# A recurrence regrouped: units of 64 tokens of four batches in place of 128 tokens of two, with the small products at fixed places

## The chip, the core and the metric

The kernel runs on one core of a Trainium2 chip, in one launch. The metric is device time in microseconds (us). The core has five engines with instruction queues of their own: TensorE (PE in the profile, its weight loads PEld) for matrix products and transposes, VectorE (DVE) and ScalarE (ACT) for elementwise work, GpSimd (POOL), and SyncE (SP), which issues most DMAs. An engine runs its instructions in program order; it waits where one needs a result that another engine or a DMA has not made yet. TensorE writes to PSUM, a small memory of eight banks; everything else lies in SBUF or in DRAM.

## The reference

Two stages: a delta-rule attention over 768 tokens (4 batches, 8 heads, head size 48), and a feed-forward layer with a squared ReLU over the 4 x 768 = 3072 tokens that come out of it.

```python
k_n = k / (np.linalg.norm(k, axis=-1, keepdims=True) + 1e-06)
state = np.zeros((B, H, D, D))                       # B, H, D = 4, 8, 48
for t in range(S):                                   # S = 768
    kt, vt, bt = (k_n[:, :, t], v[:, :, t], beta[:, :, t, None])
    y[:, :, t] = np.einsum('bhd,bhde->bhe', q[:, :, t], state)
    v_old = np.einsum('bhde,bhd->bhe', state, kt)
    state = state + bt[:, :, :, None] * np.einsum('bhd,bhe->bhde', kt, vt - v_old)

x = y.transpose(0, 2, 1, 3).reshape(B * S, H * D)    # 3072 x 384
h = np.maximum(x @ w_in, 0.0)                        # w_in 384 x 2048
out = (h * h) @ w_out                                # w_out 2048 x 384
```

All data is float32. The tokens of one batch depend on one another through the state (48 x 48 a head and batch); batches and heads are independent, and the feed-forward layer needs only the rows of its own tokens.

## The kernel before, in words

**The recurrence in chunks.** 64 tokens are taken at once. With K, Q, V of a chunk and the state S at its start, the kernel forms the products K K^T and Q K^T (masked to the strict triangle), solves a unit triangular system for U from V - K S, and then has y = Q S + (masked Q K^T) U and S + K^T U. The triangular matrix is inverted in two blocks of 32 tokens: both diagonal blocks by elimination on VectorE, the block below them by two small products.

**Units.** A unit is a piece of 256 token rows on which all of this is done at once; there are twelve. Before, a unit is 128 tokens of two batches: two chunks one after the other (c = 0, 1), and units of the two batch pairs take turns (u // 2 is the token tile, u % 2 the pair), with a state tile for each pair. Rows of a tile are 2 batches x 64 tokens or, where heads stand there, 2 heads x 64.

**The parts of a unit.** Each is a Python generator that issues instructions up to its next `yield`:
- `loads`: DMAs of keys, queries, beta and values for units ahead, and the norm of the keys (`normalize`, L277 on ScalarE, L278 on VectorE);
- `static`: transposes of keys and queries on TensorE (L324) and their copies by ScalarE to `kq` (L327); the products (L340), masked by VectorE into `ap` (L350); the diagonal blocks out to DRAM (`blocks`, L358) and back in another layout (`lt`, L366), on SyncE's queue;
- `invert`: 31 rounds of two VectorE instructions (L429, L430) on `lt` and `z`, one factor at the end (L432), then `z` out to DRAM (`inv`, L436) and back into the tiles `tt` (L445) and `t1t` (L450);
- `whole`: the two small products that make the inverse's lower block (L468, L476), with a VectorE transpose of `t1t` (L461) ahead and ScalarE copies behind (L470, L480);
- `sequential`, for each of the two chunks: the products of keys and queries with the state (L498); V - K S on VectorE (L501); the inverse times that (L509), copied by ScalarE (L512); K^T U (L520), added to the state by VectorE (L523), and (Q K^T) U (L528), copied by ScalarE to `y` (L531);
- `moe`: the feed-forward stream of the unit's 256 rows. `y` is transposed on TensorE (L545) and split into a high part `x_h` (ScalarE, L550) and a low part `x_l` (VectorE, L551). Then come steps: nine products of 256 columns into `h` (L581: high x high, high x low, low x high), ReLU, square and high part on ScalarE (L588, L589, L591), the low part `h_l` on VectorE (L560), and steps of six products of 384 columns into `o` (L568). 16 steps of the first and 16 of the second kind make a unit.

Weights come in as float32 and are split once into a high and a low half (`split_weights`: steps on ScalarE, GpSimd, VectorE, two small sums on TensorE, L170 and L171, and a ScalarE copy, L172). 28 pieces of weights are split in the first units, between the other work.

**The order of the work.** The program writes the order of every engine out by hand. Units 0 and 1 are prepared together at the start, with weights split in between; then the loop over u = 1 to 11 issues, mixed with one another by `weave`, the state part of unit u (`whole`, then `sequential`), the stream of unit u - 1, `static` and `invert` for unit u + 1 and the loads of u + 2. `weave` gives the n steps of each part places between two fractions a and b of the unit, sorts all and takes them in turn; between two parts that are not marked "quiet" it pulls one step of the stream ahead:

```python
for x, (gen, n, a, b, *_) in enumerate(parts):
    order += [(a + (b - a) * (m + 0.5) / n, x) for m in range(n)]
...
    if x != filler and not quiet and not apart and filler in order:
        order.remove(filler)
        next(parts[filler][0], None)
```

`invert` is quiet and spreads over 0.40 to 1.12, that is into the next unit. Three steps of a stream (OVER), its copy and its output are left over to the next unit.

PSUM has two banks `g` (the state's products and, in turn, a pair for the transposes and products), two `x` (all other small products; in units 0 and 1 in turn with `h`), two `h` (L581 and the transposes of `y`) and two `o`.

## Time and profile before

| | |
|---|---|
| runs (us) | 688.55, 691.68, 691.93; median 691.68 |
| profiled execution (us) | 693.1, of it the span of the instructions 691.2 |
| granted TensorE clock, mean | 0.96 |
| TensorE busy | 612.2 us, 89% of the span, 9900 products |
| VectorE busy | 435.6 us, 63%, 1175 instructions |
| ScalarE busy | 322.8 us, 47%, 644 instructions |
| GpSimd busy | 75.1 us, 11% |
| DMA | 49.92 MB in 173725 packets |

The profile is one execution, taken by the hardware. A group of instructions is named by its line in the program, its engine and its operation, with out <- in by tile names; then stand the busy time, the mean duration of one in ns and the idle time of that engine just ahead of the group, with what ended it. Rows in order of time start with the time in us from the start of the span and the duration. Products overlap in TensorE's pipeline, so durations of neighbours may overlap too: the pace is read from the starts. "PEclk" is the clock that TensorE was granted, as a share of full speed.

### The profile page before, as it was taken

Reading aid. Unit: us, or ns where it says so; the run is one execution under the profiler, and the core shown is the slowest. Engines: PE = TensorE matmul, PEld = TensorE weight load, DVE = VectorE, ACT = ScalarE, POOL = GpSimd, SP = SyncE. Lnnn points to the kernel's source line nnn. Section 1 sums busy time; section 2 is a strip of 40 time slices with the busy share of each in tenths; the row PEclk is TensorE's granted clock in tenths of the full one; section 3 lists DMA queues with packets and bytes.
Section 4 is the critical chain, followed back from the end, with each engine's and each line's share of the span. In section 5 each row is a group of like instructions: output and inputs, shape, how many; then the busy total and the mean of one; then the engine's idle time right before and its main releaser. Section 6 shows DMA issues by size and latency. Waiting matters only on the chain. (4 is left out here: it accounts for less than half of the span.)

```text
span 691.2 us, 23095 instructions
## 1 busy us (share of the span) xinstructions
PE 612.2 (89%) x9900; PEld 557.1 (81%) x9900; DVE 435.6 (63%) x1175; ACT 322.8 (47%) x644; POOL 75.1 (11%) x90
## 2 busy tenths in 40 slices
PE   0850887879999999999999999999999999999997
PEld 0530456769998988989999989889889899999997
DVE  4789875897468377487486594683774874741121
ACT  3630564753643544544445535435445444454352
POOL 7531431220100100101001001001001010000000
PEclk9966797998999999999999999999999999999999
DMA  7698620500350441531422513505315314030000
GB/s 157 147 222 313 174 45 11 101 8 2 63 113 8 90 90 18 105 60 30 100 53 47 115 22 59 114 9 109 72 18 103 63 30 103 3 62 3 24 1 24
DMA packets 173725, 49.92 MB, mean 72 GB/s; under 512 B 165424, under 2 KB 168504, under 8 KB 173624
## 3 DMA queue, kind: packets, MB, share of 16 engines
q1 hardware_dynamic: 171160, 47.85, 32.8%
q8 instruction: 78, 1.28, 0.8%
q10 hardware_dynamic: 2336, 0.59, 0.4%
q14 instruction: 23, 0.19, 0.1%
q0 software_dynamic: 128, 0.01, 0.0%
HBM read 37.32 MB, written 11.01 MB: 70 GB/s over the span
## 5 line engine op out<-in xcount | busy, mean ns | idle before, releaser
L568 PE MATMUL o<-w,h_h 128*128 128x384 f32 x768 | 204.7, 348 | 0.0
L581 PE MATMUL h<-x_h,w 128*128 128x256 f32 x1152 | 176.2, 289 | 7.5 <-DVE x_l L551 6.1
L560 DVE TENSOR_TENSOR h_l<-r,h_h 128x512 fp32r<-128x512 f32 x96 | 66.6, 694 | 155.6 <-PE o L568 70.4
L581 PEld LDWEIGHTS h<-x_h,w 128*128 128x128 f32 x1152 | 154.6, 191 | 11.8 <-ACT kq L327 5.6
L568 PEld LDWEIGHTS o<-w,h_h 128*128 128x128 f32 x768 | 133.2, 189 | 3.3
L568 PE MATMUL o<-w,h_l 128*128 128x384 f32 x384 | 130.1, 339 | 0.0
L588 ACT ACTIVATE r<-h 128x512 f32<-128x512 f32 x96 | 57.5, 599 | 129.8 <-PE h L581 129.7
L429 DVE SCALAR_TENSOR_TENSOR tmp<-lt,bt,z 128x126 f32<-128x126 f32 (+22 forms) x310 | 95.7, 309 | 26.1 <-DMA lt<-blocks 13.7
L581 PE MATMUL h<-x_l,w 128*128 128x256 f32 x576 | 100.2, 283 | 0.0
L430 DVE TENSOR_TENSOR z<-z,tmp 128x126 f32<-128x126 f32 (+22 forms) x310 | 79.2, 256 | 10.7
L581 PEld LDWEIGHTS h<-x_l,w 128*128 128x128 f32 x576 | 82.8, 191 | 0.0
L568 PEld LDWEIGHTS o<-w,h_l 128*128 128x128 f32 x384 | 72.6, 189 | 0.0
L589 ACT ACTIVATE r<-r 128x512 f32<-128x512 f32 x96 | 60.8, 633 | 3.1
L591 ACT CAST h_h<-r 128x512 fp32r<-128x512 f32 x96 | 59.6, 621 | 3.1
L413 POOL MEMSET z<- 128x512 f32 x10 | 5.3, 531 | 400.9 <-DMA inv<-z 400.9
L512 ACT COPY r<-x 128x192 f32<-128x192 f32 x46 | 12.6, 324 | 72.2 <-PE x L509 72.2
L143 POOL TENSOR_SCALAR a<-a 128x384 f32<-128x384 f32 (+1 forms) x19 | 27.2, 1434 | 49.6 <-ACT a L142 45.0
L550 ACT CAST x_h<-h 128x384 fp32r<-128x384 f32 x24 | 10.4, 486 | 39.8 <-PE h L545 39.8
L498 PEld LDWEIGHTS g<-state,kq 48*64 48x64 f32 x1408 | 23.3, 138 | 5.5 <-issue 5.5
L170 PE MATMUL o<-r,plus 128*128 128x512 f32 (+1 forms) x16 | 10.7, 761 | 17.5 <-DVE r L153 17.5
L509 PEld LDWEIGHTS x<-vt,tt 64*64 64x64 f32 x736 | 15.4, 134 | 13.3 <-issue 8.4
L498 PE MATMUL g<-state,kq 48*64 48x48 f32 x1408 | 26.1, 224 | 0.0
(131 smaller groups left out, 715.2 us busy)
## 6 DMA issues: line engine op xcount, KB each, us to landing
w<-in_moe_w_in_dram SPq DMA_DIRECT2D x12, 512.0 KB
w<-in_moe_w_out_dram SPq DMA_DIRECT2D x16, 384.0 KB
lt<-blocks SPq DMA_DIRECT2D x22, 256.0 KB
vt<-in_v_dram SPq DMA_DIRECT2D x48, 96.0 KB
out_dram<-a SPq DMA_DIRECT2D x46, 96.0 KB
kpad<-in_k_dram SPq DMA_DIRECT2D x88, 48.0 KB
qpad<-in_q_dram SPq DMA_DIRECT2D x88, 48.0 KB
blocks<-ap SPq DMA_DIRECT2D x48, 64.0 KB
```

The costliest lines, as they stand in the source:

```text
L143: nc.gpsimd.tensor_scalar(out=a.bitcast(F32), in0=a.bitcast(F32), scalar1=LEAST, scalar2=None, op0=ALU.max)
L429: nc.vector.scalar_tensor_tensor(out=tmp, scalar=bt[:, s:s + 1], op0=ALU.mult, op1=ALU.mult, **factors)
L430: nc.vector.tensor_tensor(out=z[:, :nj, s + 1:], in0=z[:, :nj, s + 1:], in1=tmp, op=ALU.subtract)
L498: nc.tensor.matmul(dst[to * C:(to + 1) * C, j, p], lhsT=kq[rows, c, p, b, x], rhs=s[rows, b, p], start=(x == 0 and p == 0), stop=False, sk ...
L509: nc.tensor.matmul(tv[j][to, p], lhsT=tt[rows, c, h], rhs=vt[rows, c, h], start=True, stop=True)
L512: nc.scalar.copy(out=uu[:, j::2], in_=tv[j])
L560: nc.vector.tensor_tensor(out=h_l, in0=r, in1=h_h.bitcast(F32), op=ALU.subtract)
L568: nc.tensor.matmul(o[i], lhsT=a[:, e, i * P:(i + 1) * P], rhs=halves["wo", ft][w], start=(ft == 0 and n == 0), stop=(ft == FT - 1 and n == 2))
L581: nc.tensor.matmul(hp[:, e], lhsT=halves["wi", (kt, ft // EACH)][w][:, f], rhs=x[:, kt], start=(n == 0), stop=(n == 3 * KT - 1))
L588: nc.scalar.activation(out=r, in_=hp, func=AF.Relu)
L589: nc.scalar.activation(out=r, in_=r, func=AF.Square)
L591: nc.scalar.copy(out=h_h, in_=r)
```

## The change

A unit becomes 64 tokens of all four batches: `u` is the chunk, and the index that counted the two chunks of a unit (c = 0, 1) now counts two batch pairs (batches 2c + b). The shapes of the tiles for keys, queries, values and products stay as they are; the two state tiles become one with a pair index, and each unit takes one step of the recurrence, in which both pairs go side by side:
- L498 now runs for both pairs at once, 64 products for queries into `g` and 64 for keys into two `x` banks, issued straight behind the first small product (L461; before L468), which goes to an `h` bank; the subtraction is two VectorE instructions of 384 columns;
- `solved` is the product with the inverse (L512) for both pairs, copied back into `vt`;
- `onward` is K^T U (L528), one addition of 384 columns for each half of the state, (Q K^T) U (L537) and two copies to `y`.

The order has fixed places: the stream's 28 steps of its own unit stand at 4/32 to 31/32, the four of the unit before at 0 to 3/32; the four steps of the state part at CHAIN (11.9, 15.9, 19.9, 23.9 of 32); `static` has its first step ahead of the unit and its second at 4.9/32; the transposes of `y` (now one step) stand ahead of everything. The rule that pulls steps ahead is gone. In unit 0 six weights are split beside the state part (2, 1, 2, 1), not seven, so one more is left to unit 1. Tokens, beta and output rows are addressed to match; output and computation are the same. Line numbers shift: L324, L327, L340, L350 become L317, L320, L333, L343; L429, L430, L432 become L422, L423, L425; L468, L476 become L461, L471; L509, L520, L528, L531 become L512, L528, L537, L541; L545, L550, L551, L560 become L554, L557, L558, L567; L568 and L581 become L575 and L588.

```diff
-    state = []
-    for i in range(NU):
-        s = const.tile([P, 2, NP, D], F32, name=f"state{i}")
-        nc.gpsimd.memset(s, 0.0)
-        state.append(s)
+    state = const.tile([P, 2, NC, NP, D], F32, name="state")
+    nc.gpsimd.memset(state, 0.0)
...
-    AHEAD = 20
+    AHEAD = 19
...
     def tokens(x, d):
-        t0, b0 = d["t0"], d["b0"]
-        return [x[b0 + b, :, t0:t0 + P, :].rearrange("h (c t) d -> t c h d", c=NC) for b in range(2)]
+        t0 = d["u"] * C
+        return [x[b::2, :, t0:t0 + C].rearrange("c h t d -> t c h d") for b in range(2)]
...
         nc.vector.transpose(out=t1, in_=d["t1t"])
         m = apool.tile([P, H, HB], F32, name="m", bufs=1)
         at = [upper, lower]
-        ps = x_tile(u)[:, :H * HB].rearrange("p (k t) -> p k t", k=H)
+        ps = ps_h.tile([P, PC], F32, name="h")[:, :H * HB].rearrange("p (k t) -> p k t", k=H)
         for h in range(H2):
             c, e = h // H, h % H
             for b in range(2):
                 nc.tensor.matmul(ps[at[h % 2][b], h // 2], lhsT=ap[lower[b], c, e, 0, :HB], rhs=tt[lower[b], c, e, HB:],
                                  start=True, stop=True)
         nc.scalar.copy(out=m, in_=ps)
+        if u:
+            on_state(d)
         yield
         ps = [x_tile(u)[:, :H * HB].rearrange("p (k t) -> p k t", k=H) for _ in range(2)]
         for h in range(H2):
...
                 nc.scalar.mul(out=right[upper[b], j, :, HB:], in_=ps[j][upper[b]], mul=-1.0)
         yield
...
-    def sequential(d):
...
+    def areas(two, n):
+        return [x[:, :NC * n * D].rearrange("p (c n e) -> p c n e", c=NC, n=n) for x in two]
+    def by_parity(x):
+        return [x.rearrange("p c (n j) e -> p j c n e", j=2)[:, j] for j in range(2)]
+    def on_state(d):
+        kq, vt = d["kq"], d["vt"]
+        d["g"] = g = ps_g.tile([P, 2, PC], F32, name="g")
+        ks = areas([x_tile() for _ in range(2)], NP)
+        for x, dst in ((1, areas([g[:, j] for j in range(2)], NP)), (0, ks)):
+            for c in range(NC):
+                for p in range(NP):
+                    for j in range(2):
+                        rows = slice(j * C, j * C + D)
+                        for b in range(2):
+                            to = slice((b ^ j) * C, ((b ^ j) + 1) * C)
+                            nc.tensor.matmul(dst[j][to, c, p], lhsT=kq[rows, c, p, b, x], rhs=state[rows, b, c, p],
+                                             start=(c == 0 and p == 0) if x else True, stop=not x, skip_group_check=True)
+        for left, old in zip(by_parity(vt), ks):
+            nc.vector.tensor_tensor(out=left, in0=left, in1=old, op=ALU.subtract)
+    def solved(d):
+        u, vt, tt = d["u"], d["vt"], ttile[d["u"] % 2]
+        tv = areas([x_tile(u) for _ in range(2)], NP)
         for c in range(NC):
...
             for h in range(H):
                 p, j = h // 2, h % 2
                 for b in range(2):
                     rows, to = slice(b * C, (b + 1) * C), slice((b ^ j) * C, ((b ^ j) + 1) * C)
...
+                    nc.tensor.matmul(tv[j][to, c, p], lhsT=tt[rows, c, h], rhs=vt[rows, c, h], start=True, stop=True)
+        for new, old in zip(by_parity(vt), tv):
+            nc.scalar.copy(out=new, in_=old)
+    def onward(d):
+        u, kp, ap, uu = (d[x] for x in ("u", "kp", "ap", "vt"))
+        g = d["g"] if u else ps_g.tile([P, 2, PC], F32, name="g")
+        gy = areas([g[:, j] for j in range(2)], NP)
+        if u < units - 1:
+            ku = areas([x_tile(u) for _ in range(2)], NP)
+            for c in range(NC):
+                for h in range(H):
+                    p, j = h // 2, h % 2
+                    for b in range(2):
+                        rows = slice(b * C, (b + 1) * C)
+                        nc.tensor.matmul(ku[b][j * C:(j + 1) * C, c, p], lhsT=kp[rows, c, h], rhs=uu[rows, c, h],
+                                         start=True, stop=True)
+            for b in range(2):
+                nc.vector.tensor_tensor(out=state[:, b], in0=state[:, b], in1=ku[b], op=ALU.add)
+        for c in range(NC):
             for h in range(H):
                 p, j = h // 2, h % 2
                 for b in range(2):
...
+                    rows, to = slice(b * C, (b + 1) * C), slice((b ^ j) * C, ((b ^ j) + 1) * C)
+                    nc.tensor.matmul(gy[j][to, c, p], lhsT=ap[rows, c, h, 1], rhs=uu[rows, c, h],
+                                     start=(u == 0 and c == 0 and p == 0), stop=True, skip_group_check=True)
+        for c in range(NC):
             y = apool.tile([P, H, D], F32, name="y", bufs=2)
...
+            nc.scalar.copy(out=y.rearrange("p (n j) e -> p j n e", j=2),
+                           in_=g[:, :, c * NP * D:(c + 1) * NP * D].rearrange("p j (n e) -> p j n e", n=NP))
             d["y"][c] = y
...
                     nc.tensor.transpose(xt[b][:, kt, i], y[rows, kt * P:(kt + 1) * P], ident[rows, rows])
-            if i == 0:
-                yield
...
+    def steps(n, a, b):
+        return [a + (b - a) * (m + 0.5) / n for m in range(n)]
     def weave(*parts):
-        order = []
-        for x, (gen, n, a, b, *_) in enumerate(parts):
-            order += [(a + (b - a) * (m + 0.5) / n, x) for m in range(n)]
-        order = [x for _, x in sorted(order)]
-        filler, apart = len(parts) - 1, True
-        while order:
-            x = order.pop(0)
-            quiet = "quiet" in parts[x][4:]
-            if x != filler and not quiet and not apart and filler in order:
-                order.remove(filler)
-                next(parts[filler][0], None)
+        order = sorted((at, x) for x, (_, places) in enumerate(parts) for at in places)
+        for _, x in order:
             next(parts[x][0], None)
-            apart = apart if quiet else x == filler
-        for gen, _, _, _, *kind in parts:
-            if not kind:
-                take(gen)
     def loads(u):
...
     def state_part(d):
         yield from whole(d)
-        yield from sequential(d)
+        solved(d)
+        yield
+        onward(d)
+        yield
     F0, F1, F2 = 3, 3, 6
-    NS = 3 * (NW + 1 - (1 + 6 + 4 + 7)) + 2
-    OVER, M0, M1, E2 = 3, 0.032, 0.97, 0.13
+    EARLY = (2, 1, 2, 1)
+    NS = 3 * (NW + 1 - (1 + 6 + 4 + sum(EARLY))) + 2
+    STEPS = 32
+    OVER = 4
+    CHAIN = (11.9, 15.9, 19.9, 23.9)
     L1, N1 = (0.22, 0.42), (0.62, 0.92)
-    A1, Q1 = (0.0, 0.22), (0.34, 0.98)
     I0, I1, NI = 0.40, 1.12, HB
-    n_moe = 34
-    units = NU * NT
+    units = S // C
...
-        for _ in state_part(ds_[0]):
-            take(splits, 1)
+        for n, _ in zip(EARLY, state_part(ds_[0])):
+            take(splits, n)
         split_early = False
         before = inverse = None
         n_i = round((1 - I0) / (I1 - I0) * NI)
         for u in range(1, units):
-            parts = [(splits, NS, 0, 0.88, "quiet")] if u == 1 else []
+            parts = []
             if inverse:
-                parts.append((inverse, NI - n_i, 0, I1 - 1, "quiet"))
-            getting = loads(u)
-            parts += [(getting, 2, *L1, "quiet"), (getting, 6, *N1, "quiet")]
+                parts.append((inverse, steps(NI - n_i, 0, I1 - 1)))
+            getting, now = loads(u), moe(ds_[u - 1])
+            parts += [(now, [-2])]
             if u < units - 1:
-                parts.append((static(ds_[u + 1]), 2, *A1))
-            parts.append((state_part(ds_[u]), 8 - (u < NU), *Q1))
-            if before:
-                parts += [(before, OVER + 1, 0, E2, ""), (before, 1, 0.2, 0.24, "quiet")]
-            before = moe(ds_[u - 1])
+                parts.append((static(ds_[u + 1]), [-1, 4.9 / STEPS]))
             inverse = invert(ds_[u + 1]) if u < units - 1 else None
             if inverse:
-                parts.append((inverse, n_i, I0, 1, "quiet"))
-            parts.append((before, n_moe - OVER, M0, M1, ""))
+                parts.append((inverse, steps(n_i, I0, 1)))
+            parts += [(getting, steps(2, *L1) + steps(6, *N1)), (state_part(ds_[u]), [x / STEPS for x in CHAIN])]
+            if u == 1:
+                parts.append((splits, steps(NS, 0, 0.88)))
+            if before:
+                parts += [(before, [x / STEPS for x in range(OVER)] + [0.2, 0.21])]
+            parts.append((now, [x / STEPS for x in range(OVER, STEPS)]))
             weave(*parts)
+            before = now
         final = moe(ds_[units - 1])
-        weave((before, OVER + 1, 0.2, 1, ""), (final, 2, 0, 0.5, ""))
+        take(final, 1)
         take(before)
         take(final)
...
```

Three places where the order moves. First TensorE, around the state's products of a unit in the middle (`tt_108` is that unit's inverse, `o_...` its predecessor's sums, `w_...` the weights). Before:

```order
L568 MATMUL o_2131<-w_816,h_l 128x384
L498 MATMUL g<-state_112,kq 64x48 x32
L568 MATMUL o_2130<-w_868,h_h 128x384 x2
...
L568 MATMUL o_2131<-w_868,h_l 128x384
L581 MATMUL h<-x_h,w_1011 128x256
...
L581 MATMUL h<-x_l,w_1096 128x256
L509 MATMUL x<-vt,tt_108 64x48 x16
```

and with the change:

```order
L575 MATMUL o_2130<-w_514,h_l 128x384
L461 MATMUL h<-tt_108,ap 32x32 x32
L498 MATMUL g<-state,kq 64x48 x32
L498 MATMUL x<-state,kq 64x48 x32
L588 MATMUL h<-x_h,w_762 128x256
...
L471 MATMUL x<-m,t_2318 32x32 x32
L588 MATMUL h<-x_h,w_985 128x256
...
L575 MATMUL o_2130<-w_866,h_l 128x384
L512 MATMUL x<-vt,tt_108 64x48 x32
```

Before, two steps of the stream stood between L498 and L509, and the pass was run twice a unit; now the state's products follow the first small product, and eight steps and the visit of L471 stand ahead of the product with the inverse.

Second VectorE, where the inverse of the next unit begins (L429 and L430, now L422 and L423). Before:

```order
L461 STREAM_TRANSPOSE t_4019<-t1t 128x256
L560 TENSOR_TENSOR h_l<-r,h_h 128x512
L429 SCALAR_TENSOR_TENSOR tmp<-lt,bt,z 128x31
L430 TENSOR_TENSOR z<-z,tmp 128x31
...
L560 TENSOR_TENSOR h_l<-r,h_h 128x512
L501 TENSOR_TENSOR vt<-vt,g 128x2x4x48
L429 SCALAR_TENSOR_TENSOR tmp<-lt,bt,z 128x100
```

and with the change:

```order
L454 STREAM_TRANSPOSE t_3954<-t1t 128x256
L501 TENSOR_TENSOR vt<-vt,x 128x8x48 x2
L422 SCALAR_TENSOR_TENSOR tmp<-lt,bt,z 128x31
L423 TENSOR_TENSOR z<-z,tmp 128x31
L422 SCALAR_TENSOR_TENSOR tmp<-lt,bt,z 128x30
L423 TENSOR_TENSOR z<-z,tmp 128x30
L567 TENSOR_TENSOR h_l<-r,h_h 128x512
```

The subtraction stood between the inverse's rows; both of its halves now stand ahead of the first row.

Third ScalarE, at the start of unit 1. Before:

```order
L531 COPY y<-g 128x2x4x48
L163 CAST w_1145<-r 128x384
L172 CAST w_1096<-o_1147 128x512
L172 CAST w_1145<-x 128x384
L142 ACTIVATE a<-w_621 128x384
L327 COPY kq<-x 128x2x4x64 x2
L327 COPY kq<-g 128x2x4x64 x2
L163 CAST w_1217<-a 128x384
L550 CAST x_h<-h 128x6x64 x2
```

and with the change:

```order
L541 COPY y<-g 128x2x4x48 x2
L158 CAST w_1084<-a 128x512
L167 CAST w_1000<-o_1086 128x512
L557 CAST x_h<-h 128x6x64 x2
L320 COPY kq<-x 128x2x4x64 x2
L320 COPY kq<-g 128x2x4x64 x2
L167 CAST w_1084<-x 128x512
```

The cast to `x_h` stood behind the copies of `kq`; now it stands ahead of them.

51 lines of the change are left out of this document (5 added, 46 removed).

## The prediction, as it was put on record

> **What bounds the kernel now.** I read the page first (busy shares, the 40 slices), then busy time unit by unit, then TensorE's instructions in order of time, then those of VectorE and of SyncE's DMA queue around what TensorE waits for. From the page, the share of TensorE, its busy tenths and its granted clock:
>
> ```profile
> PE 612.2 (89%) x9900; PEld 557.1 (81%) x9900; DVE 435.6 (63%) x1175; ACT 322.8 (47%) x644; POOL 75.1 (11%) x90
> ...
> PE   0850887879999999999999999999999999999997
> ...
> PEclk9966797998999999999999999999999999999999
> ```
>
> The program has two parts. In the first ten slices (173 us) TensorE has gaps and a lowered clock; after that it is full at clock 1. Cut at the first transpose of each unit's keys, the full part gives this (the first unit, the last with a neighbour ahead of it, and the tail):
>
> ```profile
> core 0: us, PE busy (x) PEld busy (x) DVE busy (x) ACT busy (x) POOL busy (x), PEclk, DMA share, GB/s
> 172.06:220.19 48.13, 47.01 (x830) 43.95 (x830) 31.89 (x95) 22.82 (x45) 1.96 (x3) 1.00 0.35 66
> ...
> 510.12:559.02 48.90, 47.01 (x829) 43.95 (x828) 31.99 (x95) 22.82 (x45) 1.96 (x3) 1.00 0.34 64
> ...
> 652.53:691.20 38.67, 34.20 (x241) 33.87 (x240) 6.65 (x10) 15.48 (x26) 0.00 (x0) 0.99 0.09 21
> ```
>
> From 172.06 to 559.02 are eight units, 48.37 us each. TensorE sets the pace there, VectorE is busy for two thirds. So what the change is worth is read from TensorE's row: what it pays beside the products themselves.
>
> **What a visit costs.** A visit is a stretch of small products between steps of the feed-forward stream. One of them in order of time:
>
> ```profile
> 427.49 0.87 PE L581 MATMUL h<-x_h,w 128*128 128x256 f32 x6
> ...
> 428.56 0.87 PE L581 MATMUL h<-x_h,w 128*128 128x256 f32 x6
> 429.27 0.52 PE L581 MATMUL h<-x_l,w 128*128 128x256 f32 x3
> 429.72 0.75 PE L468 MATMUL x<-tt,ap 32*32 32x32 f32 x64
> 430.40 0.62 PE L568 MATMUL o<-w,h_h 128*128 128x384 f32 x2
> 430.86 0.34 PE L568 MATMUL o<-w,h_l 128*128 128x384 f32 x1
> 431.03 0.52 PE L568 MATMUL o<-w,h_h 128*128 128x384 f32 x2
> 431.39 0.34 PE L568 MATMUL o<-w,h_l 128*128 128x384 f32 x1
> ```
>
> Durations overlap, so I go by starts. A step of nine takes 428.56 - 427.49 = 1.07, so the stream would have gone on at 429.63; the visit starts at 429.72, 0.09 late. Behind it the first pair takes 430.86 - 430.40 = 0.46 to the next row, against 431.39 - 431.03 = 0.36 in the stream: 0.10. A visit costs 0.19 us beside its products. The number of products is the same in the change (a chunk of a batch pair becomes a pair of a unit, and both skip the same first and last ones).
>
> In the order of before a full unit has 11 visits: two of L545 (the second together with L324), L340, L468, L476, and twice L498, L509 and L520 with L528. In the change it has 6. The last unit has 12 with the tail's two, and 6. Nine units are full (the eight and the next one). Removed: 9 x 5 + 6 = 51 visits, x 0.19 = **9.7 us**. Bounds: 0 if two small groups side by side pay as two visits do, 9.7 if the seam is free; I take 9.7, since L520 and L528 follow one another without a gap.
>
> The Trainium skill's page TensorEngine Tiling (Array Packing), section Tiling Modes, Key Properties, says that changing the tiling mode, and not only the tile, drains TensorE. The two halves above agree with it: 128*128 to 32*32 and back. By that rule the new visit of L461 and L498 keeps one change inside (32*32 to 64*64), which would take 11 x 0.10 = 1.1 us off the gain; no row here has such a seam, and the sum leaves it out.
>
> **The waits.** Two groups of rows by form hold nearly all idle time of TensorE in the full part, with one row of the start and one typical wait:
>
> ```profile
> L581 PE MATMUL h<-x_h,w 128*128 128x256 f32 x1152 | 176.2, 289 | 7.5 <-DVE x_l L551 6.1 <-ACT kq L327 1.4
> L509 PE MATMUL x<-vt,tt 64*64 64x48 f32 x736 | 18.3, 223 | 8.5 <-DVE tmp L429 5.0 <-DVE vt L501 2.6 <-DMA kpad<-in_k_dram 0.5
> ...
> 107.06 1.62 PE L581 MATMUL h<-x_h,w 128*128 128x256 f32 x6 [2.90 <-DVE x_l L551]
> ...
> 403.29 0.87 PE L581 MATMUL h<-x_h,w 128*128 128x256 f32 x6
> 403.99 0.51 PE L581 MATMUL h<-x_l,w 128*128 128x256 f32 x3
> 404.77 0.68 PE L509 MATMUL x<-vt,tt 64*64 64x48 f32 x32 [0.26 <-DVE vt L501]
> ```
>
> Without the 2.90 of the start, 8.5 + 7.5 - 2.9 = 13.1 us. Each is a reader set too close behind its writer. L509 stands two steps (2.1 us) behind L498, while the subtraction on VectorE queues behind the inverse's rows; L581 stands straight behind the transposes, while x_l is still being made. In the change L512 stands eight steps behind L498 (two pairs of two, the visit of L471, two pairs more), and four steps of the old unit stand between the transposes and the first row of the new stream: 8.5 and 4.2 us at 1.06 a step. The waits go. By starts they are a little longer than printed: 403.29 + 1.07 + 0.09 = 404.45 against 404.77 is 0.32, not 0.26; three a unit at 0.06 over ten units add 1.8. Together **14.9 us**. Bounds: 7.5 if half come back elsewhere, 14.9.
>
> If every one goes, a unit is 48.37 less 5 x 0.19 and less about 1.5, **45.9 us** or a little under on TensorE.
>
> **What is late next.** VectorE and SyncE run a ring from unit to unit: the inverse's last row, its way through DRAM into tt and t1t, then blocks out and lt back, all one behind the other on SyncE's queue, then the first row of the next inverse. One turn, VectorE and queue:
>
> ```profile
> 387.00 0.25 DVE L429 SCALAR_TENSOR_TENSOR tmp<-lt,bt,z 128x31 f32<-128x31 f32 x1 [1.64 <-DMA lt<-blocks]
> 391.10 0.69 DVE L560 TENSOR_TENSOR h_l<-r,h_h 128x512 fp32r<-128x512 f32 x1 [0.74 <-PE o L568]
> 396.97 0.56 DVE L278 TENSOR_REDUCE n<-rest 128x8 f32<-128x384 f32 x1 [1.47 <-ACT rest L277]
> 403.56 0.69 DVE L560 TENSOR_TENSOR h_l<-r,h_h 128x512 fp32r<-128x512 f32 x1 [0.39 <-PE o L568]
> 404.17 0.55 DVE L501 TENSOR_TENSOR vt<-vt,g 128x384 f32<-128x384 f32 x1
> 416.89 0.69 DVE L432 TENSOR_TENSOR z<-z,bt 128x512 f32<-128x512 f32 x1
> ...
> 417.64 1.27 SPq L436 DMA_DIRECT2D inv<-z  x2
> 430.36 1.14 SPq L366 DMA_DIRECT2D lt<-blocks  x2
> ...
> 435.15 0.25 DVE L429 SCALAR_TENSOR_TENSOR tmp<-lt,bt,z 128x31 f32<-128x31 f32 x1 [1.58 <-DMA lt<-blocks]
> ```
>
> From 387.00 to 417.58 VectorE takes 30.6 us, from there to 435.15 the DMAs take 17.6: 48.15, the whole unit. Inside stand 0.74 + 1.47 + 0.39 = 2.6 us in which VectorE waits for others. In the change both subtractions (about 1.0) move ahead of the ring's first row, and one more h_l (0.6) falls inside it. Floor: 48.15 - 2.6 - 1.0 + 0.6 = **45.2 us** if no idle time is left, 47.8 if all of it is. So the ring is as long as TensorE's unit. There is some room before TensorE feels it (the first reader of tt, the L468 of 429.72, starts 12.1 us behind the way out at 417.64, and h_l is wanted several steps after it is made), which is used up if the ring is the longer one. I take 46.2 for it, 0.3 a unit over TensorE: **3 us given back** over nine units. Bounds: 0, and 17 (9 x 1.9) at 47.8.
>
> VectorE's and ScalarE's own work falls (one state addition of 384 columns for two of 192, one copy for two), beside other work: nothing. SyncE's queue keeps its order.
>
> **The start.** The first state part, unit 1 and the weights that are left:
>
> ```profile
> 80.00:100.00 20.00, 18.58 (x368) 11.70 (x358) 16.00 (x34) 13.24 (x31) 9.21 (x6) 0.85 0.38 65
> ...
> 87.06 0.91 PE L170 MATMUL o<-a,plus 128*128 128x384 f32 x2
> 88.30 0.83 PE L520 MATMUL h<-r,kpad 64*64 64x48 f32 x30
> 90.79 1.15 PE L498 MATMUL g<-state,kq 48*64 48x48 f32 x64
> ...
> 103.48 1.07 ACT L327 COPY kq<-x 128x512 f32<-128x512 f32 x2 [0.36 <-PE x L324]
> 105.80 0.89 ACT L550 CAST x_h<-h 128x384 fp32r<-128x384 f32 x2
> ...
> 150.00:160.00 10.00, 6.44 (x82) 6.08 (x83) 9.06 (x25) 3.61 (x8) 0.00 (x0) 0.72 0.01 2
> ...
> 152.96 0.55 DVE L177 TENSOR_TENSOR w<-a,w 128x384 fp32r<-128x384 f32 x1
> 153.56 0.45 PE L170 MATMUL x<-w,plus 128*128 128x384 f32 x1 [3.58 <-DVE w L177]
> 155.28 0.55 DVE L278 TENSOR_REDUCE n<-r 128x8 f32<-128x384 f32 x1
> ```
>
> The first state part has TensorE 93% busy. It loses one weight (88.30 - 87.06 = 1.24), L498 (1.1) and two visits (0.4): -2.7, between 0 (VectorE's 80% deciding) and -4. Behind it x_h stands ahead of the kq copies on ScalarE, no longer 105.80 - 103.48 = 2.3 us behind their start: -2.3 of the 2.90 above. Unit 1 gets these back: a weight more, 155.28 - 152.96 = 2.3 on a VectorE that is full there, L498's 1.1, less four visits (0.8): +2.6. Sum **-2.4**, between -7 and +4.
>
> The Trainium skill's page TensorE: Matmul & The Clock Gate, section HAM oscillation, has TensorE's clock fall when it idles longer than about 3.4 us. The 3.58 above with the clock of 0.72 in its row agrees; were the extra weight to lift another wait over that mark, half a window (an estimate from the page: 1.7 us) would be lost. It lies inside the bound of +4.
>
> **Sum.** -9.7 - 14.9 + 3 - 2.4 = -24.0. The profiled execution took 693.1 us for a span of 691.2 and would take 669.1; the runs' median of 691.68 is 1.4 below it: **667.6 us**.
>
> **Rivals.**
> A, the ring keeps most of its idle time and decides, 47 to 47.8 a unit: 9 x 1.1 to 9 x 1.9 over TensorE's 45.9 in place of the 3, 675 to 682. For it: VectorE is strictly one row behind another, and ScalarE's row that it waits 1.47 for keeps its place. Against it: what waits for TensorE's pace inside the ring shrinks with that pace.
> B, the seams cost as much as the visits did: only waits go, -14.9 + 3 - 2.4, 677. For it: nothing of before shows L461 beside L498. Against it: L520 beside L528.
> C, slower: the ring's DMA part grows, as transfers are packed into shorter units and SyncE reaches blocks later. From 48.4 a turn it takes more than the unit of before, so it decides once the DMA part is over 17.6 + 0.6 with all idle time kept; with 19.5 it is 49.7, 9 x 1.3 = 12 more than before, 2 less by the start and 2 in the last unit: 700. Against it: DMA engines are busy a third of these units.
> D, better: the ring takes nothing and the start gains its 7: -31.6, 660, or a little less.
>
> **Chances.** The forecast (660 to 674) 0.66, A 0.14, B 0.08, C 0.04, D 0.06, no change (a start that eats what the units gain) 0.02. The range, 656 to 682, holds all but C; its lower end lies 4 us under D, 0.4 a unit, half of what the units of before differ by (48.13 to 48.90). Half a per cent, 3.4 us, is about what can be told from no change here: faster 0.93, same 0.03, slower 0.04.
>
> **What would show it.** Right: six visits a unit, no printed idle on L512 and at most 1 us on the first L588 in the full part, a unit of 45.5 to 46.5. The ring: an idle row of VectorE for lt above 1.6 and growing, or TensorE waiting for tt or t1t at L461 or L471. The seam: L498's first rows late by 0.1 or more behind L461. Wrong: units of 48, or a first key transpose of unit 2 later than 172.

## The result, and the profile after

Four runs of the change gave 664.12 to 669.49 us, median **668.62**; the kernel before, on the same chips, 690.37. The ratio is **0.967** (95% interval 0.962 to 0.973). The profiled execution took 668.09 us with a span of 666.0. Forecast were 667.6 us, 656 to 682.

The total is where it was forecast. Not all of its parts are, and most of what follows is about that. First the page of the change, TensorE's shares and its clock:

```profile
PE 593.1 (89%) x9898; PEld 551.7 (83%) x9898; DVE 434.7 (65%) x1154; ACT 319.3 (48%) x620; POOL 73.7 (11%) x89
...
PEclk9965788788999999999899999999999999999999
```

TensorE's share is 89% as before: its busy time fell by 19.1 us and its idle time by 6.1. Cut at the same places as before (first transpose of keys in unit 1, in unit 2, in the last unit that has them, end), before and then the change; the first column is the stretch, the second its length, the last but two the clock:

```profile
102.30:172.29 69.99, 58.03 (x790) 53.32 (x788) 52.54 (x131) 36.89 (x74) 12.31 (x9) 0.88 0.16 30
172.29:559.26 386.97, 375.85 (x6630) 351.46 (x6628) 255.89 (x752) 182.50 (x360) 15.66 (x24) 1.00 0.35 65
559.26:691.20 131.94, 125.58 (x1716) 119.06 (x1712) 48.07 (x120) 58.43 (x108) 1.96 (x3) 1.00 0.16 33
```

```profile
95.00:162.65 67.65, 55.92 (x836) 51.16 (x834) 54.94 (x130) 38.82 (x77) 13.41 (x10) 0.87 0.17 31
162.65:534.77 372.12, 365.16 (x6631) 349.94 (x6628) 253.04 (x735) 180.80 (x344) 16.09 (x24) 1.00 0.36 68
534.77:666.00 131.23, 125.37 (x1734) 121.39 (x1730) 51.13 (x129) 57.70 (x104) 1.96 (x3) 0.99 0.16 33
```

The cuts do not divide the work alike. At the cut in unit 2 one step of the old unit's stream is still to come before, and four in the change (90 and 72 of its 96 products into `o` are done), and so it is at the last cut. The last stretch with the products of L568 (L575 in the change) alone, before and then the change:

```profile
559.26:691.20 131.94, 57.78 (x294) 50.46 (x294) 1.00 0.16 33
```

```profile
534.77:666.00 131.23, 58.79 (x312) 54.13 (x312) 0.99 0.16 33
```

The 18 products more are three steps of 1.06 us, 3.2 us in all. At equal work the end is shorter by them and the start longer:

| stretch | before | change | difference | at equal work | forecast |
|---|---|---|---|---|---|
| up to unit 2 (the start) | 172.29 | 162.65 | -9.6 | -6.4 | -2.4 |
| eight units | 386.97 | 372.12 | -14.9 | -14.9 | -17.4 (8 x 2.17) |
| from there to the end | 131.94 | 131.23 | -0.7 | -3.9 | -4.2 |

A unit takes 46.5 us on average. The two groups that held the idle time of before are clean, and a new one is not (groups of TensorE by form; the last column is idle time ahead of the group):

```profile
L588 PE MATMUL h<-x_h,w 128*128 128x256 f32 x1152 | 177.4, 290 | 0.0
L512 PE MATMUL x<-vt,tt 64*64 64x48 f32 x704 | 14.8, 224 | 0.0
L498 PE MATMUL x<-state,kq 48*64 48x48 f32 x704 | 14.1, 221 | 7.2 <-issue 7.2
```

"issue" means that TensorE waited for nothing that the profile shows. In order of time, the idle rows of TensorE in the full part:

```profile
227.80 0.78 PE L498 MATMUL x<-state,kq 48*64 48x48 f32 x35 [1.39 <-issue]
300.93 0.53 PE L317 MATMUL x<-plus,kpad 64*128 64x64 f32 x8 [0.89 <-DVE kpad L283]
321.54 0.84 PE L498 MATMUL x<-state,kq 48*64 48x48 f32 x41 [2.04 <-issue]
395.95 0.53 PE L317 MATMUL x<-plus,kpad 64*128 64x64 f32 x8 [0.62 <-DVE kpad L283]
415.15 0.91 PE L498 MATMUL x<-state,kq 48*64 48x48 f32 x47 [0.69 <-issue]
488.36 0.53 PE L317 MATMUL x<-plus,kpad 64*128 64x64 f32 x8 [0.59 <-DVE kpad L283]
507.49 1.02 PE L498 MATMUL x<-state,kq 48*64 48x48 f32 x53 [0.75 <-issue]
```

Two patterns take turns. In one unit TensorE stops inside the merged visit, with 35, 41, 47, 53 of its 192 products left; in the next it waits at the keys' transposes for VectorE's norm. Two units by their windows (from one L461 to the next), one without a wait and the longest:

```profile
178.94:224.13 45.19, 45.19 (x829) 43.43 (x828) 31.71 (x92) 22.57 (x43) 1.96 (x3) 1.00 0.34 66
...
317.32:366.30 48.98, 46.94 (x830) 45.05 (x829) 31.87 (x92) 22.57 (x43) 1.96 (x3) 0.97 0.34 64
```

TensorE alone needs 45.19, less than the 45.9 of the forecast. The wait of 2.04 made a unit 3.8 us longer, because the clock fell behind it (0.97).

### The profile page after: what moved, and what is told of

The parts are those of the page before. It is cut to its first block, busy times and chain, and to the rows that moved or that the text cites. A ratio compares the mean times of both kernels' runs of the same rounds, so it can differ in the third digit from the quotient of the medians.

```text
span 666.0 us, 23091 instructions
## 1 busy us (share of the span) xinstructions
PE 593.1 (89%) x9898; PEld 551.7 (83%) x9898; DVE 434.7 (65%) x1154; ACT 319.3 (48%) x620; POOL 73.7 (11%) x89
## 3 DMA queue, kind: packets, MB, share of 16 engines
q8 instruction: 78, 1.28, 0.8%
## 4 chain that ended last, share of the span: by engine, by line
PE 61%; DVE 19%; DMA 9%; SPq 4%; issue 4%; ACT 2%; DVEq 0%; ACTq 0%
PE h L588 24%; PE o L575 23%; DVE tmp L422 4%; DVE z L423 3%; DMA kpad<-in_k_dram 2%; DVE tt L423 2%; DVE h_h L420 2%; DVE h_l L567 2%; PE x L498 2%; PE g L498 1%; DMA blocks<-ap 1%; DMA inv<-z 1%; PE g L333 1%; DMA lt<-blocks 1%; PE x L333 1%
## 5 line engine op out<-in xcount | busy, mean ns | idle before, releaser
L575 PE MATMUL o<-w,h_h 128*128 128x384 f32 x768 | 200.0, 342 | 0.0
L588 PE MATMUL h<-x_h,w 128*128 128x256 f32 x1152 | 177.4, 290 | 0.0
L588 PEld LDWEIGHTS h<-x_h,w 128*128 128x128 f32 x1152 | 155.1, 193 | 3.6 <-issue 0.2
L575 PEld LDWEIGHTS o<-w,h_h 128*128 128x128 f32 x768 | 136.3, 189 | 0.8
L567 DVE TENSOR_TENSOR h_l<-r,h_h 128x512 fp32r<-128x512 f32 x96 | 67.1, 699 | 99.1 <-PE o L575 61.2
L575 PE MATMUL o<-w,h_l 128*128 128x384 f32 x384 | 130.4, 340 | 0.0
L422 DVE SCALAR_TENSOR_TENSOR tmp<-lt,bt,z 128x126 f32<-128x126 f32 (+22 forms) x310 | 95.5, 308 | 50.7 <-DMA lt<-blocks 44.0
L588 PE MATMUL h<-x_l,w 128*128 128x256 f32 x576 | 100.9, 284 | 0.6 <-issue 0.6
L423 DVE TENSOR_TENSOR z<-z,tmp 128x126 f32<-128x126 f32 (+22 forms) x310 | 79.2, 255 | 10.7
L588 PEld LDWEIGHTS h<-x_l,w 128*128 128x128 f32 x576 | 83.2, 192 | 0.8 <-issue 0.8
L575 PEld LDWEIGHTS o<-w,h_l 128*128 128x128 f32 x384 | 72.5, 189 | 0.0
L138 POOL TENSOR_SCALAR a<-a 128x384 f32<-128x384 f32 (+1 forms) x19 | 26.2, 1380 | 50.4 <-ACT a L137 46.5
L165 PE MATMUL o<-r,plus 128*128 128x512 f32 (+1 forms) x16 | 10.5, 745 | 18.6 <-DVE r L148 18.6
L501 DVE TENSOR_TENSOR vt<-vt,x 128x384 f32<-128x384 f32 x22 | 11.2, 549 | 15.2 <-PE x L498 15.2
L475 ACT ACTIVATE tt<-x 32x256 f32<-32x256 f32 x44 | 16.5, 374 | 9.6 <-PE x L471 9.0
L317 PE MATMUL x<-plus,kpad 64*128 64x64 f32 x104 | 7.8, 248 | 14.5 <-DMA kpad<-in_k_dram 12.4
L498 PE MATMUL x<-state,kq 48*64 48x48 f32 x704 | 14.1, 221 | 7.2 <-issue 7.2
L165 PEld LDWEIGHTS o<-r,plus 128*128 128x128 f32 x16 | 3.0, 234 | 20.2 <-ACT s L273 18.2
```

The source lines that it names most:

```text
L138: nc.gpsimd.tensor_scalar(out=a.bitcast(F32), in0=a.bitcast(F32), scalar1=LEAST, scalar2=None, op0=ALU.max)
L165: nc.tensor.matmul(ps, lhsT=m, rhs=y, start=(m is first[0][0]), stop=False)
L422: nc.vector.scalar_tensor_tensor(out=tmp, scalar=bt[:, s:s + 1], op0=ALU.mult, op1=ALU.mult, **factors)
L423: nc.vector.tensor_tensor(out=z[:, :nj, s + 1:], in0=z[:, :nj, s + 1:], in1=tmp, op=ALU.subtract)
L475: nc.scalar.mul(out=right[upper[b], j, :, HB:], in_=ps[j][upper[b]], mul=-1.0)
L498: nc.tensor.matmul(dst[j][to, c, p], lhsT=kq[rows, c, p, b, x], rhs=state[rows, b, c, p], start=(c == 0 and p == 0) if x else True, stop=n ...
```

## Two theories for the new waits

**Instructions arrive late.** The queue for instructions (DMA queues of the change's page: packets, MB, share):

```profile
q8 instruction: 78, 1.28, 0.8%
```

That is 16.4 KB a packet; all 23091 instructions of the program take 1.28 + 0.20 MB in two such queues, 64 bytes each, so a packet holds 256. This queue is TensorE's: 78 packets of 256 are 19968 instructions, and its 9898 products with as many weight loads are 19796 of them. A product with its weight load is two, so a packet lasts 128 products. The counts fit: in a run of 192, products left 35, 41, 47, 53 are places 157, 151, 145, 139; a packet that ended 128 earlier ended at 29, 23, 17, 11, inside the same run. The steps of -6 in two units fit too, for a unit holds 1670 instructions in the trace (828 products, as many weight loads and 14 of semaphores): 2 x 1670 - 13 x 256 = 12 instructions. So the run uses up one packet before the next has come. From the end of one packet to that of the next, 128 products, TensorE works for 1.95 us; with the wait that makes 2.6 to 4.0 us until the next packet can be used. The Trainium skill, Runtime: NRT & Kernel Launch, section Instruction fetch mechanics, has blocks of 16 KiB or 256 instructions, the next one fetched while one runs, with the cost mostly hidden. The size agrees with the trace; hidden it is not, where 384 instructions pass in 2.7 us (a run without a wait, from the start of L461 to the stream's next row).

**The rival:** a wait inside L498 for its banks or for the state, which belongs to the work of every second unit.

**The ring.** VectorE's idle time ahead of the inverse's first row was 1.4 to 3.1 us before; in the change it is longer:

```profile
402.37 0.69 DVE L425 TENSOR_TENSOR z<-z,bt 128x512 f32<-128x512 f32 x1
...
403.13 1.29 SPq L429 DMA_DIRECT2D inv<-z  x2
407.68 1.91 SPq L438 DMA_DIRECT2D tt<-inv  x4
409.64 1.97 SPq L443 DMA_DIRECT2D t1t<-inv  x4
411.70 3.55 SPq L351 DMA_DIRECT2D blocks<-ap  x4
416.97 1.14 SPq L359 DMA_DIRECT2D lt<-blocks  x2
...
421.70 0.25 DVE L422 SCALAR_TENSOR_TENSOR tmp<-lt,bt,z 128x31 f32<-128x31 f32 x1 [4.60 <-DMA lt<-blocks]
```

From the inverse's end (403.06) to its next first row are 18.6 us; from its own first row, at 376.03, to its end VectorE takes 27.0. That is 45.7 for this turn, and the eight turns take 46.9 on average. If this ring sets the pace, a unit cannot be shorter than such a turn, whatever TensorE saves.

## Experiments

**e_split: no run of small products over 128.** The queries' half of L498 moves behind L471.

```diff
         if u:
-            on_state(d)
+            on_state(d, 0)          # keys, behind L461
         yield
...
+        if u:
+            on_state(d, 1)          # queries, behind L471
         yield
```

> The change with one thing moved: the 64 products of the queries with the state leave the visit of L461 and stand behind L471 instead. Still six visits a unit, but no run of small products is longer than 128 (before the edit one is 64 + 64 + 64 = 192). Fetch theory: TensorE's instructions arrive in blocks of 256 (78 packets of 16 KB in the queue for instructions, 64 bytes each), one block ahead; 192 products are 384 instructions in 2.9 us, two block ends can fall into them, and TensorE waits for the block that is not there yet (the 7.2 us ahead of L498 put down to issue, 0.62 at a first step behind, 1.7 lost to a clock of 0.97 in the unit from 317 to 366). With 128 in a run no printed wait of that kind over 0.3 us is left. The time then goes by the ring of VectorE and SyncE's queue: if the ring holds a unit at 46.2, only what the longest units (46.87 and 48.98) and unit 1 have over that comes back, about 5 us, 663 to 664; if it does not, units fall to 45.2 to 45.6 and the time to 659 to 660. Rival, a wait inside L498 for its PSUM banks or the state, which the profile cannot name: the rows of L498 on keys keep it wherever they stand, 7 us stay, 668 to 669.

664.74 us (0.962 of before; 0.960 to 0.964). No wait put down to issue of 0.2 us or more is left behind 95 us, and the rows on keys have none: the rival falls. The gain is small, as the ring theory had it, because the other wait is now in five of eight units:

```profile
160.88:531.62 370.74, 365.97 (x6630) 350.39 (x6626) 253.01 (x737) 180.77 (x346) 16.33 (x24) 1.00 0.36 68
253.46:300.52 47.06, 47.06 (x830) 45.23 (x830) 31.86 (x93) 21.80 (x41) 1.96 (x3) 0.96 0.35 67
...
253.46 0.53 PE L317 MATMUL x<-plus,kpad 64*128 64x64 f32 x8 [1.84 <-DVE kpad L283]
...
418.56 0.25 DVE L422 SCALAR_TENSOR_TENSOR tmp<-lt,bt,z 128x31 f32<-128x31 f32 x1 [6.44 <-DMA lt<-blocks]
```

370.74 over eight is 46.34 a unit, from 45.24 to 47.34; the two longest are the one that ends in the wait of 1.84 and the one behind it, in which the clock is lowered.

**e_shift: the same kernel, 96 instructions later.**

```diff
-            transposed([(c, 0) for c in range(NC)], [x_tile(u) for _ in range(2)], kq[:, :, :, :, 0])
+            for _ in range(4 if u == 0 else 1):
+                transposed([(c, 0) for c in range(NC)], [x_tile(u) for _ in range(2)], kq[:, :, :, :, 0])
```

> The change with 48 more transposes of the keys of unit 0 (the same ones four times over), at about 12 us, where TensorE waits for loads anyway. Nothing else moves; only the count of TensorE's instructions ahead of everything that follows grows by 96. Fetch theory: block ends fall 48 products earlier in each visit. In the units from 224, 317, 412 and 504 us the wait now stands with 35, 41, 47 and 53 products of L498 left, that is 157 to 139 into the run of 192, so a block ended 29 to 11 into it; these waits go. The units between them (179, 271, 366, 458, 551), in which a block now ends 96 to 72 into the run, would have it at 48 to 24 and the next 176 to 152 into it: they get the wait, with 16, 22, 28, 34 and 40 products left, 0.5 to 2 us each. The total is the same, 666 to 670. Rival, a wait for banks, data or DMA that belongs to the work of every second unit: it stays in the units from 224, 317, 412 and 504, with the same products left.

The waits in the full part moved to the other units, with 17, 23, 29, 35 and 41 products left where 16, 22, 28, 34 and 40 were forecast (L499 is L498 here):

```profile
186.52 0.45 PE L499 MATMUL x<-state,kq 48*64 48x48 f32 x17 [1.64 <-issue]
280.95 0.56 PE L499 MATMUL x<-state,kq 48*64 48x48 f32 x23 [1.41 <-issue]
374.79 0.70 PE L499 MATMUL x<-state,kq 48*64 48x48 f32 x29 [1.59 <-issue]
469.08 0.78 PE L499 MATMUL x<-state,kq 48*64 48x48 f32 x35 [1.98 <-issue]
563.85 0.80 PE L499 MATMUL x<-state,kq 48*64 48x48 f32 x41 [1.20 <-issue]
```

That settles where the wait comes from. The traces say it to the instruction: in the change and in e_early7, e_shift, e_both, e_ring and e_both_shift below, all 32 waits put down to issue behind 95 us (0.2 us or more) stand after TensorE's instruction number 256 n + 193, counted from its first record. They end 1.2 to 1.8 us after a packet of this queue has landed: in the unit from 317.32 the packet begins at 319.01 and has landed at 319.95, and TensorE goes on at 321.54.

The time, 679.1 us (0.983; 0.980 to 0.986), is about 10 above the forecast and above the change: 5.4 of it stand ahead of 100.37, where the keys' transposes of unit 1 begin (95.00 in the change), which I had taken for free and whose cause stays open, and the eight units take 378.02 instead of 372.12, with a clock of 0.96 to 0.97 in three of them.

**e_places: fixed places alone,** with the units of before.

```diff
+    CHAIN = (11.9, 14.4, 16.9, 19.9, 22.1, 24.9, 27.9, 29.9)
...
-            parts.append((state_part(ds_[u]), 8 - (u < NU), *Q1))
...
+            parts += [(getting, steps(2, *L1) + steps(6, *N1)), (state_part(ds_[u]), [x / STEPS for x in (CHAIN if u >= NU else CHAIN[:2] + CHAIN[3:])])]
```

> The kernel before (units of 128 tokens of two batches, two steps of the recurrence a unit) with fixed places alone: the eight steps of its state part at 11.9, 14.4, 16.9, 19.9, 22.1, 24.9, 27.9 and 29.9 of 32, the transposes of y together ahead of the unit, four old steps behind them. Ten visits a unit instead of eleven; L509 stands three steps behind L498 instead of two, L581 four steps behind the transposes. By the prediction's terms: the waits go (14.9 us), one visit a unit (0.19 x 10 = 1.9), x_h ahead of kq at the start (2.3), and the ring, into which the subtractions still fall, gives back 0 to 9: 672 to 681 against 690, 675 the middle. The rest to the change, 4 to 10 us, is then the regrouping. Rival: two chains in one unit cannot keep their distance, and the waits come back at L520 behind its copy or at L545 behind y: 684 or more.

679.62 us (0.983; 0.978 to 0.987): in the range, for another reason. The eight units take 387.12 us, as before (386.97). The gain is in the start and in the end: unit 2 begins at 159.21 instead of 172.29, which at equal work (this kernel too has 18 products fewer ahead of the cut) is 9.9 us. Units of 46.8 take turns with units of 48.8 to 51.0, in which this happens:

```profile
231.86 0.25 DVE L429 SCALAR_TENSOR_TENSOR tmp<-lt,bt,z 128x31 f32<-128x31 f32 x1 [8.35 <-DMA lt<-blocks]
235.60 0.55 DVE L501 TENSOR_TENSOR vt<-vt,g 128x384 f32<-128x384 f32 x1
...
236.25 0.79 PE L509 MATMUL x<-vt,tt 64*64 64x48 f32 x32 [2.37 <-issue]
```

The subtraction stands behind the inverse's first rows, they wait for lt, and L509 follows 0.1 us after the subtraction's end. The profile says issue; the order says L501, and the last packet of instructions had landed over 6 us before each of the four waits of this kind. So three steps of distance did not help a reader whose writer waits in the ring.

**e_early7: the weight back in unit 0.**

```diff
-    AHEAD = 19
+    AHEAD = 20
...
-    EARLY = (2, 1, 2, 1)
+    EARLY = (2, 2, 2, 1)
```

> The change with seven weights split beside the first state part again (2, 2, 2, 1), so one less is left to unit 1. By the prediction the first state part grows by 1.2 us and unit 1 loses 2.3: the stretch from the first L461 to the first step of the stream, 22.95 us in the change, becomes 24.2, and from there to the keys' transposes of unit 2, 63.07, becomes 60.8; the time 667.5. Rival: unit 1 is not paced by VectorE, a weight in it costs TensorE's own 0.6 us or nothing, and the time is 669 to 670 with the second stretch at 62.5 to 63.

666.75 us (0.966; 0.962 to 0.970), not told apart from the change. The first stretch is 25.16 us, the second 61.74, against 22.95 and 63.07. Both have a wait for instructions in the second (2.34 and 2.02), so a weight in unit 1 costs about 1.7, and in the first state part up to 2.2, though that stretch is 24.08 in e_split with six weights too. The move of the weight is worth nothing that can be measured.

**e_both: the run split as in e_split, and the ring's order changed.** The blocks go out ahead of tt and t1t on SyncE's queue, and the state part stands one step of the stream later, since tt then lands later.

```diff
-        from_blocks(to_blocks())
+        to_blocks()
+        yield
+        from_blocks(blocks)
         yield
...                                   # invert(), behind the way out of inv
+        if not both:
+            yield
...
-    CHAIN = (11.9, 15.9, 19.9, 23.9)
+    CHAIN = (12.9, 16.9, 20.9, 24.9)
...
-                parts.append((inverse, steps(NI - n_i, 0, I1 - 1)))
+                parts.append((inverse, steps(NI - n_i, 0, I1 - 1) + [4.92 / STEPS]))
...
-                parts.append((static(ds_[u + 1]), [-1, 4.9 / STEPS]))
+                parts.append((static(ds_[u + 1]), [-1, 4.9 / STEPS, 4.94 / STEPS]))
```

> The kernel of e_split (no run of small products over 128) with the ring's way through DRAM reordered: on SyncE's queue the blocks of the next unit go out while the inverse is still on its way to DRAM, ahead of tt and t1t, not behind them; lt stays behind them. The four steps of the state part stand one step of the stream later (12.9, 16.9, 20.9, 24.9), since tt now lands later by the two issues moved ahead of it. Ring theory: without the waits for instructions a unit of e_split takes 46.34 us on average (370.74 over eight), because VectorE waits 6.5 us for lt in each and is then late with the keys' norm, for which TensorE waits (0.6 to 1.84 us in five of eight units, once with a clock of 0.96 behind it). lt comes about 2.5 us earlier here, the waits at the keys' transposes go, and a unit falls to the 45.2 of units in which TensorE never waits: 8 to 9 us less over the program, 655 to 658. Rival: 46.3 is what TensorE itself needs in most units and the ring only fills the rest: 663 to 666, unchanged. A second rival: tt is now late for the first small product, and what is won at the keys is lost there (idle rows of 1 to 2 us on tt): 664 or more.

**655.66 us** (0.950; 0.947 to 0.953), as forecast, and better than both kernels. TensorE has 0.8 us of idle time in the eight units, which take 364.08 (one wait for instructions, with ten products of a run of 128 left); seven of them 45.3 to 45.4 each.

```profile
157.91:521.99 364.08, 363.29 (x6631) 352.37 (x6628) 254.76 (x737) 181.01 (x344) 16.59 (x24) 1.00 0.37 69
...
L424 DVE SCALAR_TENSOR_TENSOR tmp<-lt,bt,z 128x126 f32<-128x126 f32 (+22 forms) x310 | 95.7, 309 | 19.3 <-DMA lt<-blocks 11.9 <-issue 0.7
```

VectorE's wait for lt is 11.9 us over the program, 44.0 in the change.

**e_ring: the ring's order alone,** with the run of 192 left as it is.

```diff
-            on_state(d, 0)
+            on_state(d)             # otherwise as e_both
```

> The change itself, with L461 and both halves of L498 together in one visit, and only the ring's way through DRAM reordered as in e_both. Ring and fetch theory together: the waits inside L498 stay (0.7 to 2 us in every second unit, about 7 us in all), but a unit without one falls from 46.2 to 45.2, and the units with one no longer have to wait for the ring as well: 663 to 666, above e_both by 6 to 9. Rival: the ring takes no part, 668 to 670.

669.97 us (0.971; 0.966 to 0.976): not the 663 to 666 that I expected. The waits at the keys are gone, as they should be, and yet the eight units take 374.30: the waits for instructions in them grew from 4.9 to 6.7 us, and the clock fell behind two of them, not one (L502 is L498 here):

```profile
323.17 0.92 PE L502 MATMUL x<-state,kq 48*64 48x48 f32 x49 [1.93 <-issue]
...
559.75 0.50 PE L592 MATMUL h<-x_h,w 128*128 128x256 f32 x2 [2.29 <-issue]
```

The second, in the unit behind the eight, stands a few products behind the run, as does one of 2.11 at 466.14. The two causes hide one another: the ring's order alone gives nothing that can be told (+1.4), the split alone -3.9, both -13.0.

**e_visits: three visits more a unit,** on e_both.

```diff
-    EARLY = (2, 1, 2, 1)
+    EARLY = (2, 1, 0, 2, 0, 1)
...
-    CHAIN = (12.9, 16.9, 20.9, 24.9)
+    CHAIN = (12.9, 16.9, 20.9, 21.9, 24.9, 25.9)    # L512 and L528/L537 in two halves
...
-                parts.append((static(ds_[u + 1]), [-1, 4.9 / STEPS, 4.94 / STEPS]))
+                parts.append((static(ds_[u + 1]), [0.5 / STEPS, 4.9 / STEPS, 4.94 / STEPS]))
```

> The kernel of e_both with three visits more a unit: one step of the stream between the transposes of y and those of keys and queries, one between the two halves of the product with the inverse, one between the state's product and that for y. Products, waits and the ring are as they are. By the prediction's price (0.19 us a visit) a unit grows by 0.57 and the program, with eleven units that have the places, by 6 us over e_both. If small groups side by side pay as two visits do, nothing changes. If the ring still sets the pace of a unit, the growth is hidden, 0 to 2 us, and the units keep their length.

666.57 us (0.965; 0.962 to 0.968). The units without a wait are 46.22 to 46.24 long against 45.32 to 45.44: 0.85 to 0.9 for three, **0.29 a visit**, not 0.19. (The start is about 7 us longer as well, where other things moved; it is no part of the price.) One half of the product with the inverse in e_visits (L520 there), and the same product whole in the change:

```profile
379.63 0.52 PE L599 MATMUL h<-x_l,w 128*128 128x256 f32 x3
380.08 0.68 PE L520 MATMUL x<-vt,tt 64*64 64x48 f32 x32
380.69 0.98 PE L599 MATMUL h<-x_h,w 128*128 128x256 f32 x6
381.51 0.51 PE L599 MATMUL h<-x_l,w 128*128 128x256 f32 x3
```

```profile
425.55 1.15 PE L512 MATMUL x<-vt,tt 64*64 64x48 f32 x64
426.63 0.97 PE L588 MATMUL h<-x_h,w 128*128 128x256 f32 x6
```

The way in (380.08 is 0.09 late) and the slow first row (0.82 to the next, not 0.71) are there as forecast. The third part I had not counted is the way out: 32 products take 0.61 to the stream's row, and 64 of them in one run 1.08, so cutting a run in two adds 2 x 0.61 - 1.08 = 0.14 inside the runs themselves.

**e_places_ring: the units of before with both cures.** e_places with the ring's order of e_both, ten visits a unit.

```diff
-    CHAIN = (11.9, 14.4, 16.9, 19.9, 22.1, 24.9, 27.9, 29.9)
+    CHAIN = (12.4, 14.9, 17.1, 20.1, 22.1, 24.9, 27.9, 29.9)   # and to_blocks, invert as in e_both
```

> The kernel of e_places (units of 128 tokens of two batches, fixed places, ten visits, no run of small products over 64) with the ring reordered as in e_both, its eight steps at 12.4, 14.9, 17.1, 20.1, 22.1, 24.9, 27.9 and 29.9. It shows what is left of the regrouping once the waits are dealt with otherwise. In e_places every second unit waits about 2.4 us ahead of the product with the inverse, because the subtraction stands behind the inverse's first row, which waits up to 8.35 us for lt; with lt 2.5 us earlier these waits should shrink to nothing. If visits are all that regrouping saves, at the 0.29 us that e_visits gave (46.23 less 45.35 over three), a unit is 45.35 + 4 x 0.29 = 46.5 and the program 10 x 1.16 = 12 us over e_both, 665 to 669. If the regrouping also removes waits that two chains in one unit cannot avoid, units stay at 47.5 or more, 675 and up.

670.78 us (0.969; 0.965 to 0.972), 2 us above the range. The waits are gone; the eight units take 374.87, 46.86 each, all between 46.74 and 46.97. Against the 45.35 of e_both that is 1.5 for four visits, 0.38 each. With both cures the regrouped program is 15 us faster by the medians; 10.8 of it stand in the eight units, the rest in the start and the end.

**e_both_shift: 96 instructions later,** the two lines of e_shift on e_both.

> The kernel of e_both with the 48 repeated transposes of e_shift at the start. Fetch theory: with no run of small products over 128, one block of 256 instructions covers any run, wherever block ends fall; the eight units from the keys' transposes of unit 2 keep their 364 us (364.08 in e_both, 372.12 in the change, 378.02 in e_shift), with waits put down to issue of under 1 us each. The start takes what it took in e_shift: the keys' transposes of unit 1 came at 100.37 there against 95.00 in the change, so some 3 to 6 us more, 658 to 662 in all. Rival: any program of this density depends on where its blocks end, and the eight units grow by 3 us or more.

660.67 us, with two runs. The total is in the range, the full part is not, and the rival of the expectation holds: 367.57 us for the eight units (159.77 to 527.34), 3.5 more than e_both, with two waits over 1 us:

```profile
369.12 0.20 PE L507 MATMUL g<-state,kq 48*64 48x48 f32 x1 [1.01 <-issue]
461.68 0.33 PE L507 MATMUL g<-state,kq 48*64 48x48 f32 x6 [1.32 <-issue]
```

One and six products are left of a run of 128: a packet ended just ahead of the run and the next one at its end. A run of 128 is no safe length: the eight units have three such waits here (the third is 0.35), one in e_both and none in e_split, against four in the change. That a fetch takes 2.6 to 4.0 us fits this, since 128 products take less.

## Why the prediction was right, and where it was not

**Visits (-9.7 forecast).** Right in kind, too small: 0.29 us each by e_visits, 0.38 by e_places_ring, so 15 to 19 us for 51, beyond the upper bound. The term was mis-sized, since I read the way in and the row behind from one visit, but not the way out of the run itself. This is most of why TensorE needs 45.19 and not 45.9.

**The seam of L461 and L498.** In the change:

```profile
458.49 0.75 PE L461 MATMUL h<-tt,ap 32*32 32x32 f32 x64
459.18 1.15 PE L498 MATMUL g<-state,kq 48*64 48x48 f32 x64
460.14 1.11 PE L498 MATMUL x<-state,kq 48*64 48x48 f32 x64
461.19 0.97 PE L588 MATMUL h<-x_h,w 128*128 128x256 f32 x6
```

L461 takes 0.69 to L498's start, as much as a visit of such products takes to the stream's next row (0.68 in the prediction's visit), while the first 64 of L498 take 0.96 and the last 64, which lead back to the stream, 1.05. So two products of one form follow one another free, and a change of form costs its way out inside a visit too. The rule of the Trainium skill, TensorEngine Tiling (Array Packing), section Tiling Modes, Key Properties, that I left out of the sum agrees with this. By these rows, 0.09 by eleven visits, the seam is worth about 1 us, an estimate.

**Waits (-14.9).** The waits that it named went: L512 and L588 (the x_h rows) have 0.0. By e_places it was not distance alone: with the subtraction left among the inverse's rows, three steps were not enough. In the change both subtractions stand ahead of the first of these rows.

**The ring (+3, a unit of 46.2).** Right in place: with its order changed (and the state part one step later), e_split's 46.34 a unit becomes 45.51 in e_both (45.35 without its one wait). Near in size, with the lowered clock of one unit in the 46.34. It showed where I had not looked: TensorE waited for the keys' norm, not for tt or t1t.

**Missing: the waits for instructions.** No rival had them. They take 4.9 us in the eight units and a clock of 0.97 in one. The step that failed is "The waits go" with its unit of 45.9 on TensorE: merging visits made a run of 384 instructions that passes in 2.7 us, and the next packet takes up to 4.0 to come. The prediction asked of the seam only what it costs between two forms, not how fast a run uses up its instructions.

**The start (-2.4, bounds -7 to +4).** At equal work -6.4, inside the bounds but 4.0 more than forecast. Of it 1.3 stand ahead of the first L461 (76.63 against 77.97). Six of the kernels above have 75.2 to 76.4 there, e_places with the units of before among them, so the runs do not show it as a gain of the regrouping. From there to the first step of the stream the change is 6.1 shorter, where -5.0 were forecast. Unit 1 is 2.2 shorter by the cut and 1.0 longer at equal work, where +2.6 were forecast. I had called VectorE full there from one window of 10 us; over the stretch it is busy for 51.29 of 65.23:

```profile
107.06:172.29 65.23, 56.35 (x746) 51.89 (x748) 51.29 (x129) 32.86 (x65) 11.14 (x8) 0.87 0.17 32
```

```profile
101.87:159.21 57.34, 47.58 (x729) 42.68 (x730) 50.32 (x123) 33.93 (x69) 11.71 (x9) 0.97 0.20 37
```

The second row is the same stretch in e_places, with as many weights and 18 products fewer: 4.7 us less at equal work, at a clock of 0.97 for 0.87. As an estimate, its 47.58 us of TensorE's work would be 53.0 at the lower clock (x 0.97 / 0.87), so the clock may be worth more here than my terms for this unit. No run changes it alone. The change has 0.86 there; what makes its unit 1 shorter than forecast by 1.6 is open.

**The last units (-4.2).** -3.9 at equal work: as forecast. Two waits for instructions are in it (0.62 and 0.37, at 555.57 and 596.36).

So the total is right by misses that cancel: the start gave 4.0 us more than forecast, the eight units 2.5 less and the last ones 0.3 less. The eight units hide two more: TensorE's busy time there fell by 10.7 where visits were to give 7.6 (8 x 5 x 0.19), and its idle time only from 11.1 to 7.0, where the waits less the ring were to give the other 9.8.

## What to carry to other kernels

Where a change packs small instructions together, ask how long the run is in instructions and how long a fetch of the next 256 takes: here 2.6 to 4.0 us, and a run of 384 in 2.7 us stalled by where its packets happened to end. When two limits lie within 1 us of one another in a unit, taking away one shows little or nothing; the order in which a DMA queue serves a ring and the length of a run were worth 0 and 4 us alone and 13 together. And price a visit by adding some and dividing, not by reading one: its own products hide a third of the cost.
